# Maxima over key partitions: VectorE's 32x32 transposes and eight guard rows in place of TensorE's transposes and two guard rows

## The chip, the core and the metric

The kernel runs on one core of a Trainium2 chip. The core has five engines that work side by side, each through its own list of instructions in order: TensorE (PE, matmuls, with its weight loads shown as PEld), VectorE (DVE), ScalarE (ACT), GpSimd (POOL) and SyncE (SP, which here only issues DMAs). Data lie in SBUF, matmul results in PSUM's eight banks. The metric is the device time of one execution in microseconds (us).

## The reference

Four batches, eight heads, 768 positions, head dimension 64. Attention is masked by buckets: six projections of each query and key give six sign bits, and a query sees the keys with the same six bits. The result goes through a feed-forward layer (called MoE in the kernel).

```python
q_bits = (np.einsum('bhsd,dk->bhsk', q, proj) > 0)      # 6 bits; the same for k
mask = q_bucket[:, :, :, None] == k_bucket[:, :, None, :]
scores = scale * np.matmul(q, k.transpose(0, 1, 3, 2))
scores = np.where(mask, scores, -1000000000.0)
scores = scores - np.max(scores, axis=-1, keepdims=True)
attn = np.exp(scores)
attn = attn / (np.sum(attn, axis=-1, keepdims=True) + 1e-09)
out = np.matmul(attn, v)                                # then, over 3072 tokens of width 512:
h = x @ w_in                                            # 512 -> 2048
return (s * np.maximum(h, 0.0) ** 2 + b) @ w_out        # 2048 -> 512
```

## The kernel before

**Tiles and stages.** The attention is cut into 96 chunks: 4 batches x 8 heads x 3 chunks of 256 queries. For a chunk the scores are computed with keys on the partitions: six tiles of 128 keys by 256 queries, which fill three PSUM banks (0 to 2, or 5 to 7 in every second chunk of the first batch). Head dimension and hash bits are contracted together, so that masked pairs come out very low. The first batch (24 chunks, `exact`) multiplies in plain fp32 (`L576`, `L641`); the other three batches split each operand into two fp32r parts (`L578`, `L612`, `L643`, `L644`), and between their matmuls stand those of the MoE of the batch before (`L723`, `L740`), which can start when all heads of a batch are done. After the last chunk the MoE is alone. While the first batch runs, ScalarE, VectorE and GpSimd also decode the MoE's weights (`decode`, 32 units).

**The maxima.** Softmax needs the largest score of each query, over all keys, thus over partitions. Per chunk:
- `L583` (VectorE) takes the maximum over the six tiles: `mx`, 128 partitions x 256 queries.
- `L589` (TensorE) turns `mx` round with two 128x128 transposes into bank 4, queries on partitions.
- `L591` (VectorE) takes the maximum along each row, negated: `nmt`, 128 x 2.
- `L593` (TensorE) transposes `nmt` into 2 rows of 128 in bank 4.
- `L600` (VectorE) writes the guard rows: 2 rows of 256 columns, row j holding the negated maxima of queries j x 128 onward and zeros elsewhere. They lie in rows 0 and 1 of `bq` (`zhl` in the first batch).
- `L612` (`L610` in the first batch) adds them to the scores in PSUM: a matmul in whose stationary operand these rows are ones (`rest`).
- `L617` (ScalarE) takes the exponential, then come the sums (`L666`) and the value matmuls.

The rows of `bq` and `ks` that the guard rows take away are carried in `lead` (`L578`) instead, whose contraction is 64 + 12 + 2 = 78 rows.

**What sets the order.** `Plan` holds each step with an engine, a cost in us, the keys that it reads and writes and a priority, and `order` plays the steps through once with these costs: on each engine the step that is ready and has the lowest priority number goes next. Attention goes ahead of the MoE's matmuls, which fill what is left. `hold(4)` and `hold(None)` enclose steps that have bank 4 to themselves: the preparation of the next head's operands (`split`, `hash_`, `both`) uses it too. `decodes` says how many weight units are to be decoded by chunk i, by `FIRST` up to the eighth chunk and `RATE` after it. The emitted lists are fixed; on the chip each engine takes its list in order and waits where a result isn't there.

Of the kernel before, what the change touches and what calls it, by code (L numbers as in the profile page):

```python
# [173 lines left out]
def lsh_attention_moe(ctx: ExitStack, tc, q, k, v, proj, w_in, w_out, s, b, out):  # L174
# [89 lines left out]
    nmt = tile_("nmt", [P, 4, 2])  # L264
# [34 lines left out]
    pjh = tile_("pjh", [P, KB + MR], F32R)  # L299
    pjl = tile_("pjl", [P, KB + MR], F32R)  # L300
# [16 lines left out]
    ones = tile_("ones", [P, 1])  # L317
# [37 lines left out]
    def decode(u, pr):  # L355
# [53 lines left out]
    def thirds(g):  # L409
        return (0,) if g == 0 else (1, 2)  # L410
# [14 lines left out]
    def prep(w, i, pr):  # L425
# [28 lines left out]
        def split(g, i, pr):  # L454
            cols, o = slice(g * HS, (g + 1) * HS), bank[:, 4, 0:HS]

            def tr():
# [4 lines left out]
            act(HS, lambda: nc.scalar.activation(aq[:, cols], o, AF.Copy, scale=qk_sb), [("b", 4, "p")], AK(x, g=thirds(g)), pr, 0.12)
            dve(HS, lambda: nc.vector.scalar_tensor_tensor(bq[:, cols], o, qk_sb, f32(aq[:, cols]), ALU.mult, ALU.subtract), [("b", 4, "p")] + AK(x, g=thirds(g)), BK(x, g=thirds(g)), pr, 0.6)
            plan.hold(None)
            if g:
                dma(lambda: ks[0:D, 0], lambda: aq[D:P], AK(x, r=(1,)), KK(x, (0,)), pr, D * S * 4)
                dma(lambda: ks[TPC:D, 1], lambda: aq[D + TPC:P], AK(x, r=(1,)), KK(x, (3,)), pr, D * S * 4)
                dma(lambda: ks[HR:HR + TPC, 0], lambda: aq[D:D + TPC], AK(x, r=(1,)), KK(x, (4,)), pr, S * 4)
                dma(lambda: ks[D:P, 1], lambda: bq[D:P], BK(x, r=(1,)), KK(x, (1,)), pr, D * S * 4)

        def hash_(g, i, pr):
# [91 lines left out]
    def scores(i, pr):  # L563
# [41 lines left out]
        for p in range(NP_):
# [163 lines left out]
    def freed(x):  # L769
# [99 lines left out]
```

## Time and profile before

| | us |
|---|---|
| median of 3 runs (lowest, highest) | 1071.52 (1070.59, 1071.64) |
| the profiled execution | 1071.75 |
| its span in the trace | 1070.0 |
| TensorE busy | 1044.6 |
| ScalarE busy | 686.3 |
| GpSimd busy | 652.0 |
| VectorE busy | 634.7 |

Busy times are of the whole span. A matmul's time in the trace is that from its start to its end, with the length of the pipeline in it, and the next one starts before it ends; what an instruction costs TensorE is read from the starts of its neighbours. Where a row merges several instructions (x2, x6), its start is that of the first.

### The profile page before, as it was taken

The numbers are of one execution on the slowest core, as the hardware profiler recorded it, in microseconds if no ns is written. First come the engines' busy times: TensorE is split into PE (matmuls) and PEld (weight loads), VectorE is DVE, ScalarE is ACT, GpSimd is POOL, SyncE is SP. The second block draws the span as 40 slices with busy tenths as digits, with TensorE's granted clock in tenths as the row PEclk, the third lists the DMA queues.
The fourth block names the chain that finished last, engine by engine and source line by source line (L and its number), as shares of the span: only waits on it lengthen the run. The fifth ranks groups of instructions, "written<-read, shape, count | busy, mean of one in ns | idle before, by whom it ended". The sixth has DMA issues, their size and how long they took to land.

```text
span 1070.0 us, 18632 instructions
## 1 busy us (share of the span) xinstructions
PE 1044.6 (98%) x6918; PEld 936.2 (87%) x6918; DVE 634.7 (59%) x750; ACT 686.3 (64%) x1355; POOL 652.0 (61%) x593
## 2 busy tenths in 40 slices
PE   8999999889999999999999999999999999999998
PEld 6888788679999989899889999999899999988997
DVE  5676878757677676757676676767676765100000
ACT  4667778857677767666767676776767677333332
POOL 2355857767667676666757775767667777322221
PEclk9999999999999999999999999999999999999999
DMA  6344445322422332331342232242242130201010
GB/s 148 102 140 131 141 140 160 98 66 51 129 75 70 96 94 55 105 94 46 73 116 76 55 119 66 71 118 73 68 114 76 46 97 11 79 1 60 9 41 20
DMA packets 91402, 89.11 MB, mean 83 GB/s; under 512 B 61760, under 2 KB 65344, under 8 KB 91312
## 3 DMA queue, kind: packets, MB, share of 16 engines
q1 hardware_dynamic: 86112, 70.88, 24.8%
q10 hardware_dynamic: 5200, 17.05, 5.1%
q8 instruction: 54, 0.88, 0.3%
q14 instruction: 36, 0.29, 0.1%
HBM read 48.24 MB, written 18.87 MB: 63 GB/s over the span
## 4 chain that ended last, share of the span: by engine, by line
PE 87%; DMA 3%; POOL 3%; ACT 3%; issue 2%; DVE 2%; ACTq 0%; SPq 0%; DVEq 0%; POOLq 0%
PE bank L723 25%; PE bank L740 23%; PE bank L644 5%; PE bank L612 5%; PE bank L643 5%; PE bank L641 4%; PE bank L578 4%; PE bank L576 4%; PE bank L589 2%; DMA xd<-xsb 2%; PE bank L674 2%; PE bank L610 1%; PE bank L459 1%; POOL hl L637 1%; DMA raw<-in_moe_w_out_dram 1%
## 5 line engine op out<-in xcount | busy, mean ns | idle before, releaser
L637 POOL TENSOR_TENSOR hl<-et,hl 128x512 fp32r<-128x512 f32 x216 | 279.1, 1319 | 139.8 <-ACT hl L636 123.1
L723 PE MATMUL bank<-xc,w 128*128 128x256 f32 x2304 | 338.7, 285 | 1.1 <-DMA xc<-xd 0.7
L723 PEld LDWEIGHTS bank<-xc,w 128*128 128x128 f32 x2304 | 305.7, 191 | 9.3 <-DMA xc<-xd 0.9
L740 PE MATMUL bank<-w,ghb 128*128 128x512 f32 x768 | 258.9, 401 | 0.0
L731 POOL TENSOR_TENSOR glb<-rb,ghb 128x512 fp32r<-128x512 f32 x96 | 124.2, 1294 | 126.5 <-ACT ghb L730 110.4
L583 DVE TENSOR_REDUCE mx<-bank 128x256 f32<-128x1536 f32 x96 | 168.1, 1751 | 16.8 <-PE bank L578 12.2
L666 DVE TENSOR_REDUCE zb<-et 128x256 f32<-128x1536 f32 x72 | 126.0, 1750 | 50.0 <-ACT et L617 32.1
L740 PE MATMUL bank<-w,glb 128*128 128x512 f32 x384 | 153.5, 401 | 0.1
L617 ACT ACTIVATE et<-bank 128x512 f32<-128x512 f32 x240 | 132.5, 624 | 32.8 <-PE bank L612 21.0
L740 PEld LDWEIGHTS bank<-w,ghb 128*128 128x128 f32 x768 | 136.3, 189 | 17.9 <-issue 0.8
L728 ACT ACTIVATE rb<-bank 128x512 f32<-128x512 f32 x96 | 57.5, 599 | 144.6 <-PE bank L723 134.7
L636 ACT CAST hl<-et 128x512 fp32r<-128x512 f32 x216 | 131.4, 667 | 0.4
L643 PE MATMUL bank<-hl,vs 128*128 128x256 f32 x432 | 118.6, 294 | 1.0 <-ACT hl L636 0.6
L644 PE MATMUL bank<-hl,vs 128*128 128x256 f32 x432 | 113.8, 282 | 1.9 <-POOL hl L637 1.9
L679 ACT ACTIVATE xpb<-bank,vmn 64x256 f32<-64x256 f32 x96 | 44.9, 468 | 74.9 <-PE bank L644 74.0
L578 PE MATMUL bank<-aq,ks 78*128 78x256 f32 x432 | 86.8, 290 | 3.2 <-DMA aq<-nat 3.1
L644 PEld LDWEIGHTS bank<-hl,vs 128*128 128x128 f32 x432 | 82.3, 191 | 7.0 <-POOL hl L637 2.5
L643 PEld LDWEIGHTS bank<-hl,vs 128*128 128x128 f32 x432 | 82.1, 190 | 6.8 <-ACT hl L636 1.0
L686 DVE RECIPROCAL zpb<-zpb 128x256 f32<-128x256 f32 x48 | 83.5, 1741 | 5.3 <-ACT zpb L677 5.3
L740 PEld LDWEIGHTS bank<-w,glb 128*128 128x128 f32 x384 | 72.4, 189 | 11.7 <-POOL glb L731 0.6
L748 DVE SCALAR_TENSOR_TENSOR osb<-bank,misc,bcs 128x512 f32<-128x512 f32 x22 | 16.1, 741 | 109.2 <-PE bank L740 109.1
L578 PEld LDWEIGHTS bank<-aq,ks 78*128 78x128 f32 x432 | 69.8, 190 | 9.8 <-ACT zhl L667 3.3
(115 smaller groups left out, 1659.5 us busy)
## 6 DMA issues: line engine op xcount, KB each, us to landing
xd<-xsb SPq DMA_DIRECT2D x48, 256.0 KB
xc<-xd SPq DMA_DIRECT2D x48, 256.0 KB
raw<-in_moe_w_in_dram ACTq DMA_DIRECT2D x16, 512.0 KB
raw<-in_moe_w_out_dram ACTq DMA_DIRECT2D x16, 512.0 KB
nat<-in_q_dram SPq DMA_DIRECT2D x32, 192.0 KB
nat<-in_k_dram SPq DMA_DIRECT2D x32, 192.0 KB
out_dram<-osb SPq DMA_DIRECT2D x22, 256.0 KB
vn<-in_v_dram SPq DMA_DIRECT2D x24, 192.0 KB
```

Source lines behind the costliest of these rows:

```text
L578: nc.tensor.matmul(o, ks[0:HR + TPC, 0, kt], aq[0:HR + TPC, cs], start=m == 0, stop=m == 1, skip_group_check=True)
L583: dve(S * TPC, lambda: nc.vector.tensor_reduce(t, sc, AX.XY, ALU.max), [("b", b) for b in pb], [tk], pr, 1.75)
L617: act(512, lambda p=p, z=z: nc.scalar.activation(et(z) if plain(i) else pairs(z), bank[:, pb[p]] if plain(i) else bank[:, pb[p]].rearrange ...
L636: act(512, lambda z=z, y=y: nc.scalar.copy(HL[2 * y].rearrange("p (m n) -> p m n", n=CH), pairs(z)), [("e", z)], [("hl", 2 * y)], pr)
L637: pool(512, lambda z=z, y=y: nc.gpsimd.tensor_tensor(HL[2 * y + 1].rearrange("p (m n) -> p m n", n=CH), pairs(z), f32(HL[2 * y]).rearrange ...
L643: nc.tensor.matmul(av, VS[w % 2][:, kt], HL[2 * y][:, ms], start=(kt == 0), stop=False)
L644: nc.tensor.matmul(av, VS[w % 2][:, kt], HL[2 * y + 1][:, ms], start=False, stop=(kt == NT - 1))
L666: dve(S * TPC, lambda: nc.vector.tensor_reduce(ZB, es, AX.XY, ALU.add), [("e", z) for z in range(NE)], ["zb"], pr, 1.75)
L686: dve(CH, lambda: nc.vector.reciprocal(zp, zp), [], zk, pr + 20, 1.75)
L723: nc.tensor.matmul(hp, wt[("wi", n, cc)][:, m % 2, fs], xc[:, m // 2, :], start=(cc == 0 and m == 0), stop=(cc == NC_ - 1 and m == 2))
L731: pool(2 * CH, lambda r=r, gh=gh, gl=gl: nc.gpsimd.tensor_tensor(gl, r, f32(gh), ALU.subtract), [rk, hk], [lk], MP)
L740: nc.tensor.matmul(bank[:, 6 + t, :], (gh, gh, gl)[n][:, ts], wt[("wo", f)][:, n % 2], start=(f == 0 and n == 0), stop=(f == NF - 1 and n ...
```

## The change

The maxima over key partitions go another way. `mx` is transposed in place on VectorE in blocks of 32x32: a block of 32 keys by 32 queries becomes 32 queries by 32 keys. A reduction over each 32 columns gives `nmt`, 128 x 8: for each of four groups of 32 key partitions and eight groups of 32 queries the maximum over the keys of the group. One TensorE transpose makes 8 rows of 128 of it, a VectorE reduction over the four groups gives `qm`, 8 x 32, negated, and the product with the identity spreads it to 8 guard rows of 256 columns. The contraction in `lead` is 64 + 12 + 8 = 84 rows. Bank 4 is held from the small transpose to the reduction behind it. Besides, the keys by which the planner knows parts of `aq` and `bq` become finer, some planned costs and `FIRST` are other numbers, and three small tiles are laid together.

```diff
-    nmt = tile_("nmt", [P, 4, 2])
+    nmt = tile_("nmt", [P, NR])
+    QM = tile_("qm", [NR, SQ])
...
-        dve(256, lambda: nc.vector.tensor_scalar(raw()[:, :, 1], gi, -2**31, None, ALU.bitwise_and), [gk], rk, pr, 0.68)
-        dve(512, lambda: nc.vector.scalar_tensor_tensor(gi, gi, 3, raw()[:, :, 1], ALU.logical_shift_left, ALU.bitwise_or), rk, [gk], pr, 1.1)
+        dve(256, lambda: nc.vector.tensor_scalar(raw()[:, :, 1], gi, -2**31, None, ALU.bitwise_and), [gk], rk, pr, 0.6)
+        dve(512, lambda: nc.vector.scalar_tensor_tensor(gi, gi, 3, raw()[:, :, 1], ALU.logical_shift_left, ALU.bitwise_or), rk, [gk], pr, 0.92)
...
-        return (0,) if g == 0 else (1, 2)
+        return (0, 1) if g == 0 else (2, 3)
+
+    CG = ((0,), (1, 2), (3,))
...
-                dma(lambda: ks[TPC:D, 1], lambda: aq[D + TPC:P], AK(x, r=(1,)), KK(x, (3,)), pr, D * S * 4)
-                dma(lambda: ks[HR:HR + TPC, 0], lambda: aq[D:D + TPC], AK(x, r=(1,)), KK(x, (4,)), pr, S * 4)
+                dma(lambda: ks[NR:D, 1], lambda: aq[D + NR:P], AK(x, r=(1,)), KK(x, (3,)), pr, D * S * 4)
+                dma(lambda: ks[HR:HR + NR, 0], lambda: aq[D:D + NR], AK(x, r=(1,)), KK(x, (4,)), pr, S * 4)
...
-                dma(lambda: aq[HR:HR + TPC], lambda: bq[0:TPC], BK(x, r=(0,)), MK(x) + AK(x, r=(1,)), pr, S * 4)
+                dma(lambda: aq[HR:HR + NR], lambda: bq[0:NR], BK(x, r=(0,)), MK(x) + AK(x, r=(1,)), pr, S * 4)
...
-                    nc.tensor.matmul(o, ks[0:HR + TPC, 0, kt], aq[0:HR + TPC, cs], start=m == 0, stop=m == 1, skip_group_check=True)
+                    nc.tensor.matmul(o, ks[0:HR + NR, 0, kt], aq[0:HR + NR, cs], start=m == 0, stop=m == 1, skip_group_check=True)
...
+        m2, m2k = MX, "mx"
+        dve(CH, lambda: nc.vector.transpose(out=m2, in_=t), [tk], [m2k], pr, 0.33)
+        dve(CH, lambda: nc.vector.tensor_reduce(nm, m2.rearrange("p (b n) -> p b n", n=SQ), AX.X, ALU.max), [m2k], [nk], pr, 0.33)
         plan.hold(4)
...
-        def across():
-            for j in range(TPC):
-                nc.tensor.transpose(out=bank[:, 4, j * P:(j + 1) * P], in_=t[:, j * P:(j + 1) * P], identity=ident)
-        pe(0.23, across, [tk], [("b", 4, "c")], pr, True)
-        dve(CH, lambda: nc.vector.tensor_reduce(nm, bank[:, 4, 0:CH].rearrange("p (j n) -> p j n", j=TPC), AX.X, ALU.max, negate=True), [("b", 4, "c")], [nk], pr, 0.41)
-
-        pe(0.115, lambda: nc.tensor.transpose(out=bank[0:TPC, 4, 0:P], in_=nm, identity=ident), [nk], [("b", 4, "c")], pr, True)
+        pe(0.115, lambda: nc.tensor.transpose(out=bank[0:NR, 4, 0:P], in_=nm, identity=ident), [nk], [("b", 4, "c")], pr, True)
+        qm, qk = QM, "qm"
+        dve(CH, lambda: nc.vector.tensor_reduce(qm, bank[0:NR, 4, 0:P].rearrange("b (k n) -> b n k", n=SQ), AX.X, ALU.max, negate=True), [("b", 4, "c")], [qk], pr, 0.26)
+        plan.hold(None)
...
-            nc.vector.scalar_tensor_tensor(mr.rearrange("p (j n) -> p j n", j=TPC), o, -FLOOR, d, ALU.min, ALU.mult)
-        dve(CH, rows, [("b", 4, "c")], [mk], pr, 0.41)
-        plan.hold(None)
+            nc.vector.scalar_tensor_tensor(mr.rearrange("p (j n) -> p j n", j=NR), o, -FLOOR, d, ALU.min, ALU.mult)
+        dve(CH, rows, [qk], [mk], pr, 0.33)
...
-FIRST = 1.4
+FIRST = 1.6
```

The lines of the changed kernel that the rows below name: `L588` is the reduction `L583`, `L590` the block transpose, `L591` the reduction to `nmt`, `L595` the small transpose, `L597` the reduction to `qm`, `L605` the guard rows, `L616` the `rest` matmul; `L727` and `L744` are the MoE's matmuls, `L647` and `L648` the value matmuls, `L678` the sum's, `L690` the reciprocal.

On TensorE, the stretch from the small transpose to the guard rows' matmuls, in the third batch (the 66th chunk), before:

```order
L593 MATMUL bank<-ident,nmt 2x128
L740 MATMUL bank<-w_1325,ghb 128x512
L740 MATMUL bank<-w_1325,glb 128x512
L740 MATMUL bank<-w_1325,ghb 128x512 x2
L612 MATMUL bank<-bq_1320,ks_1496 128x256 x6
```

The same stretch of the same chunk in the changed kernel:

```order
L595 MATMUL bank<-ident,nmt 8x128
L727 MATMUL bank<-xc_1_2_4956,w_1422 128x256 x3
L727 MATMUL bank<-xc_1_3_4966,w_1434 128x256 x2
L678 MATMUL bank<-zhl,oner 128x256 x2
L727 MATMUL bank<-xc_1_3_4966,w_1434 128x256
L616 MATMUL bank<-bq_1337,ks_1518 128x256 x6
```

Four 512-column matmuls stood between the two; now eight of 256 columns do. The two transposes `L589` ahead of them are gone from the list.

On VectorE, the same chunk before:

```order
L583 TENSOR_REDUCE mx<-bank 128x256
L686 RECIPROCAL zpb<-zpb 128x256
L591 TENSOR_REDUCE nmt<-bank 128x2
L681 TENSOR_TENSOR xpb<-xpb,bank 64x256
L600 SCALAR_TENSOR_TENSOR bq_1320<-bank,ident 2x256
```

And in the changed kernel:

```order
L588 TENSOR_REDUCE mx<-bank 128x256
L590 STREAM_TRANSPOSE mx<-mx 128x256
L591 TENSOR_REDUCE nmt<-mx 128x8
L690 RECIPROCAL zpb<-zpb 128x256
L468 SCALAR_TENSOR_TENSOR bq_1337<-bank,misc,aq_1336 128x384
L685 TENSOR_TENSOR xpb<-xpb,bank 64x256
L597 TENSOR_REDUCE qm<-bank 8x32
L605 SCALAR_TENSOR_TENSOR bq_1337<-qm,ident 8x256
```

The reciprocal stood between the maxima and the reduction to `nmt`, where TensorE's two transposes ran; now it stands behind that reduction, with two other operations, where the small transpose runs.

On POOL, the end of the weights' decoding (`L377`, `L384`, `L385`) and the first low half of the second batch (`L637`), before:

```order
L377 TENSOR_TENSOR osb<-osb,raw_235 128x512
L385 TENSOR_TENSOR w_1610<-osb,w_1610 128x512
L687 TENSOR_TENSOR xpb<-xpb,zpb 128x256
L385 TENSOR_TENSOR w_1633<-osb,w_1633 128x512
L689 TENSOR_TENSOR xsb<-xpb,xsb 128x256
L384 TENSOR_TENSOR bcs<-bcs,osb 128x512
L637 TENSOR_TENSOR hl_1567<-et,hl_1561 128x512
```

And in the changed kernel, where the same operations are `L380`, `L387`, `L388` and `L641`:

```order
L387 TENSOR_TENSOR bcs<-bcs,osb 128x512
L691 TENSOR_TENSOR xpb<-xpb,zpb 128x256
L388 TENSOR_TENSOR w_1584<-osb,w_1584 128x512
L693 TENSOR_TENSOR xsb<-xpb,xsb 128x256
L691 TENSOR_TENSOR xpb<-xpb,zpb 128x256
L693 TENSOR_TENSOR xsb<-xpb,xsb 128x256
L691 TENSOR_TENSOR xpb<-xpb,zpb 128x256
L641 TENSOR_TENSOR hl_1575<-et,hl_1569 128x512
```

The last decode stood directly ahead of the first low half; now four other operations stand between.

## Rows read from the trace of the kernel before

**Rows 1.** The page: the line of part 1 (busy us, share of the span, instructions), and part 4, the chain that ended last by engine.

```profile
PE 1044.6 (98%) x6918; PEld 936.2 (87%) x6918; DVE 634.7 (59%) x750; ACT 686.3 (64%) x1355; POOL 652.0 (61%) x593
...
PE 87%; DMA 3%; POOL 3%; ACT 3%; issue 2%; DVE 2%; ACTq 0%; SPq 0%; DVEq 0%; POOLq 0%
```

**Rows 2.** Busy time of each engine by stage: start and end, length, then PE, PEld, DVE, ACT, POOL (instructions in brackets), the granted clock, DMA share and GB/s.

```profile
0.00:205.00 205.00, 194.92 (x1055) 161.22 (x1055) 148.26 (x213) 144.95 (x285) 117.67 (x106) 1.00 0.48 136
205.00:900.00 695.00, 683.30 (x4811) 625.31 (x4812) 473.95 (x521) 481.95 (x971) 488.13 (x450) 1.00 0.30 80
900.00:1070.00 170.00, 166.38 (x1056) 149.66 (x1054) 12.53 (x16) 59.37 (x100) 46.16 (x39) 1.00 0.10 35
```

**Rows 3.** Groups of instructions by line and shape: busy us and mean ns of one, then the idle time before them and what ended it.

```profile
L583 DVE TENSOR_REDUCE mx<-bank 128x256 f32<-128x1536 f32 x96 | 168.1, 1751 | 16.8 <-PE bank L578 12.2 <-PE bank L576 2.9 <-ACT hl L636 0.5
L666 DVE TENSOR_REDUCE zb<-et 128x256 f32<-128x1536 f32 x72 | 126.0, 1750 | 50.0 <-ACT et L617 32.1 <-ACT vmn L510 11.5 <-ACT zpb L677 3.0
L686 DVE RECIPROCAL zpb<-zpb 128x256 f32<-128x256 f32 x48 | 83.5, 1741 | 5.3 <-ACT zpb L677 5.3
L591 DVE TENSOR_REDUCE nmt<-bank 128x2 f32<-128x256 f32 x96 | 39.6, 412 | 57.3 <-PE bank L589 55.0 <-ACT zpb L677 2.1
L589 PE MATMUL bank<-ident,mx 128*128 128x128 f32 x192 | 37.3, 276 | 3.5 <-DVE mx L583 1.2 <-ACT hl L636 1.1 <-DVE bq L463 1.0
L600 DVE SCALAR_TENSOR_TENSOR bq<-bank,ident 2x256 fp32r<-2x256 f32 x72 | 29.4, 409 | 32.0 <-PE bank L593 31.5
L600 DVE SCALAR_TENSOR_TENSOR zhl<-bank,ident 2x256 fp32r<-2x256 f32 x24 | 9.8, 408 | 8.7 <-PE bank L593 8.2
L322 DVE CAST zhl<-zb 128x256 fp32r<-128x256 f32 x2 | 1.7, 858 | 0.0
L320 DVE MEMSET zb<- 128x256 f32 x1 | 0.3, 272 | 0.0
```

**Rows 4.** TensorE's instructions in order of time in two chunks of the third batch: start, us from start to end, line, count.

```profile
601.56 0.27 PE L593 MATMUL bank<-ident,nmt 128*2 128x128 f32 x1
...
609.40 0.28 PE L643 MATMUL bank<-hl,vs 128*128 128x256 f32 x1
609.52 0.28 PE L644 MATMUL bank<-hl,vs 128*128 128x256 f32 x1
609.64 0.38 PE L589 MATMUL bank<-ident,mx 128*128 128x128 f32 x2
609.78 0.36 PE L643 MATMUL bank<-hl,vs 128*128 128x256 f32 x1
609.98 0.28 PE L644 MATMUL bank<-hl,vs 128*128 128x256 f32 x1
...
611.97 0.27 PE L593 MATMUL bank<-ident,nmt 128*2 128x128 f32 x1
612.00 0.48 PE L740 MATMUL bank<-w,ghb 128*128 128x512 f32 x1
612.32 0.40 PE L740 MATMUL bank<-w,glb 128*128 128x512 f32 x1
612.55 0.63 PE L740 MATMUL bank<-w,ghb 128*128 128x512 f32 x2
```

**Rows 5.** VectorE's instructions in the same two chunks.

```profile
601.87 0.41 DVE L600 SCALAR_TENSOR_TENSOR bq<-bank,ident 2x256 fp32r<-2x256 f32 x1 [0.19 <-PE bank L593]
...
607.53 1.74 DVE L583 TENSOR_REDUCE mx<-bank 128x256 f32<-128x1536 f32 x1
...
610.86 0.35 DVE L591 TENSOR_REDUCE nmt<-bank 128x2 f32<-128x256 f32 x1
611.97 0.42 DVE L681 TENSOR_TENSOR xpb<-xpb,bank 64x256 f32<-64x256 f32 x1 [0.75 <-ACT xpb L679]
612.42 0.41 DVE L600 SCALAR_TENSOR_TENSOR bq<-bank,ident 2x256 fp32r<-2x256 f32 x1
```

**Rows 6.** The waits of TensorE's weight loads: who waited for whom, us in total, times, longest.

```profile
PEld bank L593 <- DVE nmt L591: 3.6, 7, 0.8
...
PEld bank L589 <- DVE mx L583: 2.3, 4, 1.3
...
PEld bank L612 <- DVE bq L600: 0.7, 3, 0.3
```

**Rows 7.** VectorE's instructions in order of time at 41 us: two of the weights' decoding, the second of which needs the first.

```profile
41.48 0.41 DVE L375 TENSOR_SCALAR raw<-osb 128x512 int32<-128x512 int32 x1
41.92 0.69 DVE L376 SCALAR_TENSOR_TENSOR osb<-osb,raw 128x512 int32<-128x512 int32 x1
```

**Rows 8.** All engines in order of time at 102 us, of which a product on VectorE and the weight load that waits for it.

```profile
102.07 0.41 DVE L600 SCALAR_TENSOR_TENSOR zhl<-bank,ident 2x256 fp32r<-2x256 f32 x1
...
102.53 0.31 PEld L445 LDWEIGHTS bank<-ident,nat 128*128 128x128 f32 x3 [0.50 <-DVE zhl L600]
```

**Rows 9.** The passage from the first to the second batch: POOL's instructions from 204 to 214 us, and the busy times from 205 to 235 us (columns as in rows 2).

```profile
204.42 1.74 POOL L377 TENSOR_TENSOR osb<-osb,raw 128x512 int32<-128x512 int32 x1 [0.83 <-DVE osb L376]
...
212.94 1.27 POOL L384 TENSOR_TENSOR bcs<-bcs,osb 128x512 f32<-128x512 f32 x1
214.16 2.60 POOL L637 TENSOR_TENSOR hl<-et,hl 128x512 fp32r<-128x512 f32 x2
...
205.00:235.00 30.00, 24.82 (x161) 21.83 (x162) 19.31 (x20) 20.12 (x41) 26.39 (x24) 0.97 0.28 72
```

More of the change, by code (lines that the diff above doesn't have):

```diff
@@ L185, in lsh_attention_moe @@
     TPC = CH // P
+    SQ = 32
+    NR = CH // SQ
     NC_ = DM // P
@@ L298, in lsh_attention_moe @@
             nc.vector.tensor_scalar(pj[rows, c:c + NBITS], pn[rows], (1.0 if i == r else -1.0) / (1.0 if i else SCALE), None, ALU.mult)
-    pjh = tile_("pjh", [P, KB + MR], F32R)
-    pjl = tile_("pjl", [P, KB + MR], F32R)
+    pjhl = tile_("pjhl", [P, 2, KB + MR], F32R)
+    pjh, pjl = pjhl[:, 0], pjhl[:, 1]
     nc.vector.tensor_copy(pjh, pj[:, 0:KB + MR])
@@ L316, in lsh_attention_moe @@
     nc.vector.memset(qk_sb[D:P], 1.0)
-    ones = tile_("ones", [P, 1])
+    ones = misc[:, 5:6]
     nc.vector.memset(ones, 1.0)
@@ L393, in bias, with AK, BK @@
         plan.hold(None)
-    def AK(x, r=(0, 1), g=(0, 1, 2)):
+    def AK(x, r=(0, 1), g=(0, 1, 2, 3)):
         return [("aq", x, i, j) for i in r for j in g]
-    def BK(x, r=(0, 1), g=(0, 1, 2)):
+    def BK(x, r=(0, 1), g=(0, 1, 2, 3)):
         return [("bq", x, i, j) for i in r for j in g]
@@ L582, in scores @@
+            pe(mmc(CH, 8 if exact else 2), lead, AK(x) + KK(x) if exact else AK(x, g=CG[c])  + KK(x, (0, 2, 4)), [("b", pb[p])], pr, True)
+        t, tk, nm, nk = MX, "mx", nmt, "nm"
         sc = bank[:, b0:b0 + NP_].rearrange("p b (m n) -> p n b m", n=CH)
         dve(S * TPC, lambda: nc.vector.tensor_reduce(t, sc, AX.XY, ALU.max), [("b", b) for b in pb], [tk], pr, 1.75)
+        m2, m2k = MX, "mx"
+        dve(CH, lambda: nc.vector.transpose(out=m2, in_=t), [tk], [m2k], pr, 0.33)
+        dve(CH, lambda: nc.vector.tensor_reduce(nm, m2.rearrange("p (b n) -> p b n", n=SQ), AX.X, ALU.max), [m2k], [nk], pr, 0.33)
@@ L600, in rows @@
-            nc.vector.scalar_tensor_tensor(mr.rearrange("p (j n) -> p j n", j=TPC), o, -FLOOR, d, ALU.min, ALU.mult)
-        dve(CH, rows, [("b", 4, "c")], [mk], pr, 0.41)
-        plan.hold(None)
+            mr = zhl[0:NR, y] if exact else bq[0:NR, cs]
+            o = qm.rearrange("p (j n) -> p j n", j=1).broadcast_to([NR, NR, SQ])
+            d = ident[0:NR, 0:NR].rearrange("p (j n) -> p j n", n=1).broadcast_to([NR, NR, SQ])
+            nc.vector.scalar_tensor_tensor(mr.rearrange("p (j n) -> p j n", j=NR), o, -FLOOR, d, ALU.min, ALU.mult)
@@ L612, in rest @@
                     nc.tensor.matmul(o, ks[:, 1, kt], bq[:, cs], start=False, stop=m == 1, skip_group_check=True)
-            pe(mmc(CH, 2), rest, [mk, tk] + ([] if exact else BK(x, g=(c,)) + KK(x, (1, 3))), [("b", pb[p])], pr, True)
+            pe(mmc(CH, 2), rest, [mk, tk] + ([] if exact else BK(x, g=CG[c]) + KK(x, (1, 3))), [("b", pb[p])], pr, True)
         ES = [(npiece[0] + p) % (NE + 2 * NHL) for p in range(NP_)] if plain(i) else list(range(NP_))
```

11 lines of the change are left out of this document (3 added, 8 removed).

## The prediction

> **What bounds the kernel.** I read the page first, its busy shares and the chain that ended last: TensorE is busy 98% of the span and 87% of the chain runs through it, 2% through VectorE [rows 1]. Then the windows by stage [rows 2]: up to 205 us (the first batch, 24 chunks) TensorE is busy 195 of 205 us and VectorE 148; from 205 to 900 us (72 chunks, with matmuls of the MoE between them) 683 of 695 and 474; from 900 us the MoE is alone, TensorE 166 of 170, VectorE 13. The granted clock is 1.00 in all three. So TensorE's queue sets the end: whatever TensorE does not have to issue between 205 and 900 us lets MoE matmuls come forward, and the lone MoE at the end gets shorter by it. VectorE matters only where TensorE, which works through its list in order, comes to an instruction whose VectorE result isn't there. That is rare now: TensorE's weight loads wait for `L583` 2.3 us in 4 cases, for `L591` 3.6 us in 7, at `L612` for `L600` 0.7 us in 3, all of 96 or 72 chunks [rows 6].
>
> **What goes from TensorE.** Two 128x128 transposes per chunk (`L589`, 192 in all [rows 3]). Their price is not the mean of 276 ns, which holds the pipeline's length, but what they push back [rows 4]: from `L589` at 609.64 to the second instruction behind it at 609.98 pass 0.34 us, of which the `L643` between takes 0.12 (as from 609.40 to 609.52). The pair costs 0.22 us. 96 x 0.22 = 21.1 us; 24 of the 96 lie in the first stage, 72 in the second (the two rows of `L600` [rows 3]). The small transpose stays (`L593`, now `L595`): 8 columns loaded in place of 2, the same 128 moved; 0.12 us in [rows 4] (611.97 to 612.32, less 0.23 for the `L740`). The scores contract over 84 rows instead of 78; `L578` and `L612` differ more than that in rows and start 0.12 us apart like all 256-column matmuls, so nothing.
>
> **What VectorE gets.** Per chunk it loses `L591` (0.41) and `L600` from PSUM (0.41) [rows 3]. It gets a 32x32-block transpose of 128x256, a reduction of 128x256 from SBUF, one of 8x128 from PSUM and a product of 8x256 from SBUF. Rows: the reductions of 1536 columns from PSUM (`L583`) and SBUF (`L666`) take the same 1.75 us, and 1.75 less 0.41 over 1280 columns is 1.05 ns a column. So 256 columns from SBUF are 0.41, 128 from PSUM 0.41 - 0.13 = 0.28, the product 0.41. No row shows the block transpose. Its ends are the fill of the same tile shape, 0.27 (`L320`), and the cast of that shape, 0.86 (`L322`); I take 0.41, what this trace's one-pass operations on 256 columns have. A VectorE operation that needs the one before it starts some 0.03 us after its end (`L375` ends at 41.89, `L376` starts at 41.92 [rows 7]). Together 1.51 for 0.82 us: +0.69 x 96 = 66 us on VectorE, 635 to 701 us, 66% of the span; in the second stage 474 + 50 of 695, 75%. TensorE hides that, as long as VectorE isn't late at the two places where TensorE needs it.
>
> **First place: from the column maxima to the small transpose.** (`L590`, new `L591`, `L595`, `L597`, `L605` and `L616` are lines of the changed kernel.) The planner is told 0.33 + 0.33 us for the transpose and the reduction; by the rows it is 0.03 + 0.41 + 0.03 + 0.41 = 0.88, late by 0.22. Queued behind `L595` on TensorE are the MoE and the value matmuls that hide everything else. In the chunk shown `L583` ends at 609.27 and TensorE takes `L589` at 609.64 [rows 4, 5], 0.37 us later, so a lateness of 0.22 would have been swallowed; the 4 waits in 96 [rows 6] say that such slack is usual. I choose 0.04 us a chunk, the whole 0.22 in one chunk of five or six.
>
> **Second place: from the small transpose to the guard row's matmuls.** Before, `L593` starts at 601.56 in the chunk before, `L600` 0.31 later at 601.87 [rows 4, 5]; it takes 0.41, and a waiting weight load goes 0.05 after its end (102.48 to 102.53 [rows 8]): 0.77 in all. The order rows put four `L740` (4 x 0.23) and the transpose's own 0.12 ahead of `L612`: 1.04, slack 0.27. After, 0.31 + 0.28 + 0.03 + 0.41 + 0.05 = 1.08 are needed, and the order rows show eight 256-column matmuls and the transpose ahead of `L616`: 9 x 0.12 = 1.08. No slack is left, so that every further tenth that VectorE is late is paid. I choose 0.05 us a chunk, an estimate. Both places: 0.09 x 96 = 8.6 us; bounds 0 (if the operations are as short as the planner has them; `L591` is 0.35 in one case [rows 5]) and 39 (the slow rival).
>
> [...]
>
> **What else.** The waits at `L589` itself, 3.5 us of TensorE [rows 3], go with it; their cause, a VectorE result that comes late, stays for `L595`, so I take 2 back (bounds 0 and 3.5). `FIRST` 1.6 decodes the MoE weights sooner. Before, POOL still decodes from 204 to 214 us in front of the first `L637` of the second batch, the first and the last of six operations in the rows, and TensorE loses 5.2 of the 30 us from 205 to 235 [rows 9]; the order rows show four other operations between the last decode (`L388`) and that first `hl` (`L641`) now, where there was none. I take 3 back (0 to 5.2). Bank 4 is held from the small transpose to the reduction only; the rows show one wait for it, `L445` behind `L600`, 0.50 us [rows 8], and it would end some tenths sooner: nothing that counts. The finer keys for the halves of `aq` and `bq` bind only the preparation of the next head, which the planner places after the chunks that read them: nothing. Of three DMAs per head on SP's queue, two carry 8 rows in place of 2 (6 x 768 x 4 bytes, 18 KB more) and one 6 rows fewer, beside copies of 196 KB: nothing.
>
> Sum: 1071.75 (the profiled execution) - 21.1 + 8.6 - 2 - 3 = 1054.2; it stands 0.2 above the median of the runs, so 1054.0.
>
> **The rivals.**
> 1. Short operations: VectorE's new operations cost what the planner has, no wait appears. 1071.5 - 21.1 - 2 - 3 = 1045. For it: the 0.35 us of `L591` at 610.86. Against: its mean of 0.41 [rows 3]. [...]
> 2. Queueing: `L597` stands on VectorE behind the reciprocal (1.74 us [rows 3]) and two more in the order rows, where `L600` stood behind one, `L681`. If one of these runs late, the bank-4 result lies there and `L616` waits. 0.15 us more a chunk: 1054 + 14 = 1068. For it: `L600` at 612.42 came 0.1 us late because of `L681` [rows 5]. Against: VectorE has a quarter of its time left.
> 3. Slower: the block transpose is slow. At 0.86 the first place needs 0.03 + 0.86 + 0.03 + 0.41 = 1.33 where the planner has 0.66, 0.67 late; less the 0.31 of slack in [rows 4, 5] (0.37 without the 0.06 of a handover) TensorE stands 0.36 at `L595` in each chunk, and 0.05 at `L616`: 0.41 x 96 = 39, which gives 1071.5 - 26 + 39 = 1084. It decides from 0.27 us of new waits a chunk, where the 26 us are eaten. For it: no row shows the operation. Against: both one-pass reductions run at 1.05 ns a column.
> [...]
> 4. No change: what TensorE saves turns into waits for the MoE's data or VectorE. TensorE's second stage has 12 us of idle in 695, so there is always an MoE matmul to take; little speaks for it.
>
> **The numbers.** Forecast 0.50 (own range 1047 to 1061), short 0.18, queueing 0.13, slower 0.14, no change 0.05. About 0.2% is what a measurement of this kernel can tell, 2 us. Faster by more: 0.50 + 0.18 + 0.13 less a little of the queueing case = 0.80; within: 0.05; slower: 0.15. The range 1042 to 1073 leaves out the slow end and a gain of all the waits.
>
> **What would show it.** Right: TensorE's work falls by 21 us and the lone MoE after the last chunk starts about as late as before (some 900 us) but is shorter; `L590` and `L591` at 0.41; TensorE waits at `L595` and `L616` some 5 to 12 us in sum; less idle of TensorE from 205 to 235. Wrong: `L590` above 0.6, or waits at these two above 26 us in sum, or a first stage that grows by more than 5 us because VectorE, 72% busy there, falls behind.

## The result, and the profile after

| | us | ratio to the kernel before, 95% interval |
|---|---|---|
| forecast | 1054.0 (1042 to 1073) | |
| changed kernel, median of 4 (lowest, highest) | 1080.25 (1079.41, 1081.46) | 1.0082 (1.0068 to 1.0097) |
| kernel before, median of 4 | 1071.58 (1070.59, 1072.36) | |

The changed kernel is slower by 8.7 us, where 17.5 us less were forecast. The first lines answer to [rows 1]: the busy times of the changed kernel, and the chain that ended last by engine and by line.

```profile
PE 1037.6 (96%) x6726; PEld 917.6 (85%) x6726; DVE 745.1 (69%) x942; ACT 687.2 (64%) x1355; POOL 657.1 (61%) x593
...
PE 69%; DVE 16%; ACT 6%; POOL 4%; issue 4%; DMA 1%; ACTq 0%; DVEq 0%; POOLq 0%
PE bank L727 21%; PE bank L744 18%; PE bank L616 5%; DVE bq L605 4%; PE bank L583 4%; PE bank L645 3%; PE bank L648 3%; PE bank L647 3%; PE bank L581 3%; DVE mx L588 3%; ACT et L621 2%; POOL hl L641 2%; DVE zb L670 1%; DVE zpb L690 1%; PE bank L614 1%
```

TensorE has 192 instructions fewer, as the change says, but the span grew: its idle time went from 25.4 us (1070.0 - 1044.6) to 42.1 (1079.7 - 1037.6). Its share of the chain fell from 87% to 69%, and 16% now run through VectorE, which had 2%: the first VectorE line among them is `L605`, the guard rows. VectorE's busy time is 110 us more, where 66 were forecast. By stage, with the columns of [rows 2]:

```profile
0.00:205.00 205.00, 191.13 (x998) 155.52 (x998) 173.93 (x262) 145.32 (x286) 125.53 (x111) 0.99 0.49 138
205.00:900.00 695.00, 671.22 (x4622) 604.34 (x4623) 557.14 (x664) 479.70 (x965) 482.20 (x442) 1.00 0.30 80
900.00:1079.70 179.70, 175.29 (x1109) 157.78 (x1107) 14.07 (x18) 62.14 (x104) 49.35 (x42) 1.00 0.09 33
```

From 205 to 900 us TensorE's idle doubled, from 11.7 to 23.8 us. The attention ends when it did (the last chunk's maxima start at 896.6 us, before at 896.1), and the lone MoE at the end is 10 us longer, where the forecast's 72 chunks of 0.22 us would have made it some 16 shorter. The groups that answer to [rows 3] (busy us and mean ns of one) say which VectorE operation grew:

```profile
L605 DVE SCALAR_TENSOR_TENSOR bq<-qm,ident 8x256 fp32r<-8x256 f32 x72 | 62.2, 863 | 2.5
L590 DVE STREAM_TRANSPOSE mx<-mx 128x256 f32<-128x256 f32 x96 | 42.7, 445 | 3.2
L591 DVE TENSOR_REDUCE nmt<-mx 128x8 f32<-128x256 f32 x96 | 40.3, 420 | 3.3
...
L597 DVE TENSOR_REDUCE qm<-bank 8x32 f32<-8x128 f32 x96 | 25.8, 268 | 31.3 <-PE bank L595 30.3
...
L605 DVE SCALAR_TENSOR_TENSOR zhl<-qm,ident 8x256 fp32r<-8x256 f32 x24 | 15.0, 623 | 0.9
```

Three of the four new operations came within 0.04 us of their price (0.41, 0.41, 0.28). The product `L605` takes 0.86 and 0.62 us on average instead of 0.41. Its line in the trace has 411 ns at the least, 925 in the median and 1599 at the most in the last three batches. The waits of TensorE's weight loads, which answer to [rows 6], are at the place that needs it:

```profile
PEld bank L616 <- DVE bq L605: 34.9, 55, 1.3
PEld bank L614 <- DVE zhl L605: 6.2, 8, 1.5
...
PEld bank L595 <- DVE nmt L591: 0.8, 4, 0.3
```

They were 0.7 at `L612` and 1.5 at `L610`, 2.2 us in all, and are 41.1 now. In part of such a wait the matmul before still runs; TensorE's own idle time at `L616` is the figure behind the bar, 20.8 us, where it was 0.0 at `L612`:

```profile
L616 PE MATMUL bank<-bq,ks 128*128 128x256 f32 x432 | 69.3, 296 | 20.8 <-DVE bq L605 20.4
```

What the product waits for is read from two chunks, VectorE's, POOL's and TensorE's instructions in order of time, of one chunk at 445 us and one at 475 us:

```profile
445.04 0.28 DVE L597 TENSOR_REDUCE qm<-bank 8x32 f32<-8x128 f32 x1 [0.67 <-PE bank L595]
445.35 1.43 DVE L605 SCALAR_TENSOR_TENSOR bq<-qm,ident 8x256 fp32r<-8x256 f32 x1
...
475.93 0.41 DVE L605 SCALAR_TENSOR_TENSOR bq<-qm,ident 8x256 fp32r<-8x256 f32 x1
...
445.22 1.28 POOL L735 TENSOR_TENSOR glb<-rb,ghb 128x512 fp32r<-128x512 f32 x1
...
474.69 0.73 POOL L672 TENSOR_TENSOR zhl<-zb,zhl 128x256 fp32r<-128x256 f32 x1
477.15 1.00 POOL L542 TENSOR_TENSOR vs<-vn,vs 128x384 fp32r<-128x384 f32 x1 [1.73 <-ACT vs L541]
...
445.65 0.28 PE L648 MATMUL bank<-hl,vs 128*128 128x256 f32 x1
446.83 0.97 PE L616 MATMUL bank<-bq,ks 128*128 128x256 f32 x6 [0.90 <-DVE bq L605]
```

At 475.93 POOL rests and the product takes 0.41. At 445.35 POOL has been in `L735` since 445.22; that ends at 446.50, the product at 446.78, 0.28 behind it. TensorE stands 0.90 us at `L616`. `L605` is not waiting for a semaphore there: its operand `qm` is done at 445.32, and its time counts as busy. It multiplies `qm` by `ident`, both in SBUF; `L600` before had one operand in PSUM and took 0.35 to 0.41 in all 96 chunks, in 67 of them beside POOL. The two chunks stand for all: in the 27 where POOL is in no instruction when the product starts, the product takes 0.411 to 0.417 us. In the other 69 it takes 0.411 to 1.599, 0.96 on average, and ends 0.27 to 0.33 us behind an instruction of POOL; in the longest cases that is the second of two.

In the chunk shown POOL is first, and 1.15 of `L735`'s 1.28 us lie in the product's 1.43. What in the chip makes the one end behind the other, the trace doesn't show; whether it hangs on where the operand lies is tried in runs 1 and 2. The trace shows the other order too, VectorE's line first and then POOL's:

```profile
865.14 0.41 DVE L605 SCALAR_TENSOR_TENSOR bq<-qm,ident 8x256 fp32r<-8x256 f32 x1
...
865.15 1.56 POOL L735 TENSOR_TENSOR glb<-rb,ghb 128x512 fp32r<-128x512 f32 x1 [0.42 <-ACT ghb L734]
```

Here the product started 0.01 us sooner and took its 0.41, and POOL's operation took 1.56. The 13 instances of `L735` that start inside a product have a median of 1.48 us, the 83 others 1.29.

The trace of before held the price already, in an operation that I had shown for another reason [rows 7]. `L376` (128x512) also has two operands in SBUF. Its group:

```profile
L376 DVE SCALAR_TENSOR_TENSOR osb<-osb,raw 128x512 int32<-128x512 int32 x32 | 28.5, 892 | 0.6
```

And VectorE and POOL in order of time around two of its instances:

```profile
46.89 1.74 DVE L376 SCALAR_TENSOR_TENSOR osb<-osb,raw 128x512 int32<-128x512 int32 x1
...
42.75 1.29 POOL L377 TENSOR_TENSOR osb<-osb,raw 128x512 int32<-128x512 int32 x1 [3.38 <-issue]
46.79 1.30 POOL L385 TENSOR_TENSOR w<-osb,w 128x512 fp32r<-128x512 f32 x1 [2.75 <-ACT w L379]
```

The instance at 41.92 in [rows 7], with POOL idle until 42.75, took 0.69; the one at 46.89, with POOL in `L385` until 48.09, took 1.74. The group's mean of 892 against that 0.69 is the mark of it.

### The profile page after: what moved, and what is told of

Its sections match the earlier page's. It is cut to its first block, busy times and chain, and to the rows that moved or that the text cites. A ratio compares the mean times of both kernels' runs of the same rounds, so it can differ in the third digit from the quotient of the medians.

```text
span 1079.7 us, 18383 instructions
## 1 busy us (share of the span) xinstructions
PE 1037.6 (96%) x6726; PEld 917.6 (85%) x6726; DVE 745.1 (69%) x942; ACT 687.2 (64%) x1355; POOL 657.1 (61%) x593
## 4 chain that ended last, share of the span: by engine, by line
PE 69%; DVE 16%; ACT 6%; POOL 4%; issue 4%; DMA 1%; ACTq 0%; DVEq 0%; POOLq 0%
PE bank L727 21%; PE bank L744 18%; PE bank L616 5%; DVE bq L605 4%; PE bank L583 4%; PE bank L645 3%; PE bank L648 3%; PE bank L647 3%; PE bank L581 3%; DVE mx L588 3%; ACT et L621 2%; POOL hl L641 2%; DVE zb L670 1%; DVE zpb L690 1%; PE bank L614 1%
## 5 line engine op out<-in xcount | busy, mean ns | idle before, releaser
L641 POOL TENSOR_TENSOR hl<-et,hl 128x512 fp32r<-128x512 f32 x216 | 279.2, 1319 | 117.2 <-ACT hl L640 94.2
L727 PE MATMUL bank<-xc,w 128*128 128x256 f32 x2304 | 331.4, 284 | 0.1
L727 PEld LDWEIGHTS bank<-xc,w 128*128 128x128 f32 x2304 | 303.8, 191 | 7.2 <-ACT rb L732 0.7
L744 PE MATMUL bank<-w,ghb 128*128 128x512 f32 x768 | 256.7, 398 | 0.0
L735 POOL TENSOR_TENSOR glb<-rb,ghb 128x512 fp32r<-128x512 f32 x96 | 126.0, 1312 | 129.8 <-ACT ghb L734 119.4
L588 DVE TENSOR_REDUCE mx<-bank 128x256 f32<-128x1536 f32 x96 | 168.1, 1751 | 4.5 <-PE bank L581 2.5
L744 PE MATMUL bank<-w,glb 128*128 128x512 f32 x384 | 152.6, 398 | 0.0
L744 PEld LDWEIGHTS bank<-w,ghb 128*128 128x128 f32 x768 | 136.3, 189 | 17.5
L648 PE MATMUL bank<-hl,vs 128*128 128x256 f32 x432 | 113.8, 284 | 2.2 <-POOL hl L641 2.0
L647 PE MATMUL bank<-hl,vs 128*128 128x256 f32 x432 | 115.1, 287 | 0.0
L648 PEld LDWEIGHTS bank<-hl,vs 128*128 128x128 f32 x432 | 81.9, 190 | 8.9 <-POOL hl L641 4.0
L616 PE MATMUL bank<-bq,ks 128*128 128x256 f32 x432 | 69.3, 296 | 20.8 <-DVE bq L605 20.4
L583 PE MATMUL bank<-aq,ks 84*128 84x256 f32 x432 | 87.4, 289 | 0.0
L690 DVE RECIPROCAL zpb<-zpb 128x256 f32<-128x256 f32 x48 | 83.6, 1742 | 5.3 <-ACT zpb L681 5.1
L616 PEld LDWEIGHTS bank<-bq,ks 128*128 128x128 f32 x432 | 56.0, 189 | 35.8 <-DVE bq L605 34.9
L647 PEld LDWEIGHTS bank<-hl,vs 128*128 128x128 f32 x432 | 81.8, 189 | 5.3 <-issue 0.2
```

Of the source, the lines that this page charges most:

```text
L583: nc.tensor.matmul(o, ks[0:HR + NR, 0, kt], aq[0:HR + NR, cs], start=m == 0, stop=m == 1, skip_group_check=True)
L616: nc.tensor.matmul(o, ks[:, 1, kt], bq[:, cs], start=False, stop=m == 1, skip_group_check=True)
L641: pool(512, lambda z=z, y=y: nc.gpsimd.tensor_tensor(HL[2 * y + 1].rearrange("p (m n) -> p m n", n=CH), pairs(z), f32(HL[2 * y]).rearrange ...
L647: nc.tensor.matmul(av, VS[w % 2][:, kt], HL[2 * y][:, ms], start=(kt == 0), stop=False)
L648: nc.tensor.matmul(av, VS[w % 2][:, kt], HL[2 * y + 1][:, ms], start=False, stop=(kt == NT - 1))
L727: nc.tensor.matmul(hp, wt[("wi", n, cc)][:, m % 2, fs], xc[:, m // 2, :], start=(cc == 0 and m == 0), stop=(cc == NC_ - 1 and m == 2))
```

## The experiments

In the diffs the lines are those of the changed kernel where nothing else is said.

**1 and 2. Where the product's operand lies.** So that no other step of the plan uses bank 4 while `qm` lies there, the hold is lengthened in both runs; then `qm` is put into PSUM in the second. The lists of all engines are the same in both.

```diff
-        ... negate=True), [("b", 4, "c")], [qk], pr, 0.26)
-        plan.hold(None)
+        ... negate=True), [], [("b", 4, "c"), qk], pr, 0.26)
...
-        dve(CH, rows, [qk], [mk], pr, 0.33)
+        dve(CH, rows, [qk, ("b", 4, "c")], [mk], pr, 0.33)
+        plan.hold(None)
```

> Control for the next run: the changed kernel, with bank 4 held until the guard rows' product is done instead of until the reduction before it; all operands stay where they are (qm in SBUF). Theory A (the product, L605, has both its tensor operands in SBUF and is held up while POOL runs one of its own tensor operations): the product stays at 0.8 us on average between 0.41 and 1.6, TensorE waits for it some 35 us at its weight loads as in the changed kernel, 1080 +- 4 us. Theory B (the chain of four VectorE operations is too long as such, wherever its operands are): the same, 1080. Theory C (how long bank 4 is held decides): a change by more than 5 us, up or down.

And for the second run also:

```diff
-        qm, qk = QM, "qm"
+        qm, qk = bank[0:NR, 4, P:P + SQ], "qm"
```

> As the control, instruction for instruction in the same order on every engine, but qm lies in bank 4 in PSUM, so that the product reads one operand from PSUM and one from SBUF, as it did before the change. Theory A: every one of the 96 products takes 0.41 us whatever POOL does, the waits of TensorE's weight loads at the guard rows' matmuls fall from 41 us to below 10, and the time to 1050 to 1056 us (the forecast's sum). Theory B: the product gets shorter, but TensorE still waits, since transpose and reduction are late by 0.2 us each chunk; the time falls by less than 10 us, to 1070 to 1078.

Measured: 1084.73 us with `qm` in SBUF (ratio to before 1.0127, 1.0097 to 1.0157), 1057.64 with `qm` in PSUM (0.9872, 0.9848 to 0.9896). The product's group in the control, then its two groups in the run with PSUM, and the waits of the weight loads there:

```profile
L604 DVE SCALAR_TENSOR_TENSOR bq<-qm,ident 8x256 fp32r<-8x256 f32 x72 | 59.9, 832 | 2.5
```

```profile
L604 DVE SCALAR_TENSOR_TENSOR bq<-bank,ident 8x256 fp32r<-8x256 f32 x72 | 29.6, 412 | 2.5
L604 DVE SCALAR_TENSOR_TENSOR zhl<-bank,ident 8x256 fp32r<-8x256 f32 x24 | 9.9, 412 | 0.9
```

```profile
PEld bank L616 <- DVE bq L604: 4.7, 15, 1.0
...
PEld bank L614 <- DVE zhl L604: 3.3, 6, 1.1
```

(`L604` is `L605` here.) With the same lists and one operand elsewhere, every product takes 0.41 us (0.411 to 0.414), the waits fall to 8.0 us and 27 us of time go. Theory A holds for the product and the waits; the time is 1.6 us above the range that it had given. The forecast's 1054 is missed by 3.6 us once the product costs what it had been given, but that nearness is in part luck, as the last paragraph of the next section shows. Theory B is not dead by this: the next runs show that the rest of the chain costs too. The longer hold by itself is not the gain; the control is slower than the changed kernel, by 4.5 us in the medians, with wide intervals, and 0.7 above the range that was expected of it.

**3. The product at its real price in the plan.**

```diff
-        dve(CH, rows, [qk], [mk], pr, 0.33)
+        dve(CH, rows, [qk], [mk], pr, 0.86)
```

> The changed kernel with the planned cost of the product at 0.86 us (its measured mean in batches two to four) instead of 0.33; operands in SBUF as in the changed kernel. If the time is lost because TensorE's list brings the guard rows' matmuls up too early (lists out of step with the chip): the list now has 0.5 us more of other matmuls ahead of them, the waits at their weight loads fall from 41 us to about 15 and the time to 1060 to 1066. If it is lost because the chain itself is longer and chunks come later, whatever the list: the waits go elsewhere and the time stays within 4 us of 1080.

Measured: 1068.46 us (0.9976, 0.9960 to 0.9992). The wait at `L616` in its trace:

```profile
PEld bank L616 <- DVE bq L605: 11.1, 24, 0.7
...
PEld bank L595 <- DVE nmt L591: 6.0, 23, 0.5
```

The product is as slow as before (mean 835 ns in the last three batches), but TensorE has other matmuls ahead, the wait falls from 34.9 to 11.1 and 12 us come back. That is about half of the 22.6 us between the changed kernel and run 2: this half comes of a list that brings `L616` up too early, and not of VectorE's time as such. It stops short of the 1060 to 1066 that was expected. Part of the wait went to the small transpose, where TensorE's loads now wait 6.0 us for `L591` instead of 0.8. That a time which swings between 0.41 and 1.6 can't be planned by one number may be the rest; no run shows that.

**4 and 8. `FIRST` alone**, in the changed kernel (1.6 to 1.4) and in the kernel before (1.4 to 1.6).

```diff
-FIRST = 1.6
+FIRST = 1.4
```

> The changed kernel with FIRST back at 1.4, all else as changed. By the forecast's term for the earlier decoding (3 us gained, bounds 0 to 5): 1083, with TensorE idle 1 to 5 us more between 205 and 235 us. If the decoding's pace is without effect: within 2 us of 1080. If it costs (decoding beside a VectorE that is fuller in the first stage, and more of POOL's operations beside the products there): 1077 or below.

> The kernel before with FIRST at 1.6 alone. No product with two operands from SBUF in the guard rows here, so the pace of decoding is seen by itself. Forecast's term: 3 us faster (0 to 5). If FIRST 1.6 costs by itself: up to 5 us slower. If it is without effect: within 2 us of the kernel before on this chip.

Measured: 1075.21 us, 5.0 below the changed kernel; and 1076.34 for the kernel before with 1.6, against 1070.87 for it on that chip (ratio 1.0049, 1.0032 to 1.0065). The term has the wrong sign in both. Busy times of 50 to 150 us of the kernel before (its passage is in [rows 9]):

```profile
50.00:150.00 100.00, 98.22 (x538) 81.75 (x536) 74.33 (x93) 76.22 (x151) 62.90 (x53) 1.00 0.45 132
```

then of 50 to 150 us and of the passage with `FIRST` 1.6:

```profile
50.00:150.00 100.00, 95.77 (x520) 79.43 (x519) 80.75 (x96) 77.06 (x152) 71.10 (x57) 1.00 0.46 142
205.00:235.00 30.00, 26.12 (x152) 22.08 (x150) 16.90 (x20) 17.57 (x39) 15.96 (x17) 0.89 0.20 58
```

The decoding now stands between 50 and 150 us, where VectorE gets 6 and POOL 8 us more, and TensorE loses 2.4. In the passage TensorE is busy 1.3 us more (24.8 to 26.1), but with 152 instructions instead of 161 and a granted clock of 0.89 instead of 0.97: the busy time per instruction is 0.172 us instead of 0.154, and this is no gain. The clock is also lower over the whole run: 0.992 to 0.995 in the four executions, 0.995 to 0.998 in the seven of the kernel before, of which those at 0.998 take some 2 us less than those at 0.995. With medians of 0.995 and 0.997, some 1.5 of the 5.5 us may be the clock; this is an estimate. The rest has no place in this reading and stays open.

In the changed kernel the passage did gain. First with `FIRST` 1.6, then with 1.4:

```profile
205.00:235.00 30.00, 27.87 (x186) 24.41 (x187) 23.91 (x28) 19.91 (x41) 16.21 (x16) 1.00 0.21 59
```

```profile
205.00:235.00 30.00, 24.25 (x148) 20.38 (x149) 21.31 (x26) 21.57 (x43) 25.94 (x24) 0.94 0.28 70
```

That is 3.6 us more for TensorE with 1.6, and 38 instructions. But the product is also slower with 1.6, 0.86 us against 0.74 in the last three batches, and the waits at the guard rows are 41.1 us against 32.5, so that this pair doesn't tell the pace of decoding from the luck of meeting POOL.

**5 to 7. `FIRST` and the plan's costs once the operand is in PSUM.** All three start from run 2; `psum14` has `FIRST` 1.4, `psum_costs` the measured costs, `psum_costs14` both.

```diff
-        dve(CH, lambda: nc.vector.transpose(out=m2, in_=t), [tk], [m2k], pr, 0.33)
+        dve(CH, lambda: nc.vector.transpose(out=m2, in_=t), [tk], [m2k], pr, 0.48)
...
-        ... AX.X, ALU.max), [m2k], [nk], pr, 0.33)
+        ... AX.X, ALU.max), [m2k], [nk], pr, 0.45)
...
-        ... negate=True), [], [("b", 4, "c"), qk], pr, 0.26)
+        ... negate=True), [], [("b", 4, "c"), qk], pr, 0.28)
...
-        dve(CH, rows, [qk, ("b", 4, "c")], [mk], pr, 0.33)
+        dve(CH, rows, [qk, ("b", 4, "c")], [mk], pr, 0.44)
```

> The run with qm in PSUM and FIRST back at 1.4. If the forecast's term for the earlier decoding holds (3 us gained): 1060 to 1062 us against 1057.6. If FIRST 1.6 costs by itself the 5 us that its undoing gave in the changed kernel: 1052 to 1054. If those 5 us came by another hit rate of the product and POOL's operations (the product's mean was 0.74 there against 0.86), they are gone now that the product takes 0.41 everywhere: within 2 us of 1057.6.

> The run with qm in PSUM, and the planner given what the trace shows: block transpose 0.48 (0.445 and the start behind it), reduction 0.45, reduction to qm 0.28, product 0.44, instead of 0.33, 0.33, 0.26, 0.33. If the remaining lateness of the chain against the list costs what the forecast has (8.6 us for both places): about 1050 us, and the waits of TensorE's weight loads at the small transpose and at the guard rows' matmuls fall from 16 us to under 6. If its list absorbs the lateness already: 1056 to 1059.

> Both: qm in PSUM, measured costs, FIRST 1.4. With the forecast's terms: 1053. With FIRST costing 5 us by itself and lateness 8: 1045. With neither of effect: 1056 to 1059.

| | `FIRST` 1.6 | `FIRST` 1.4 |
|---|---|---|
| planned costs as in the change | 1057.64 | 1056.55 |
| measured costs | 1041.22 | 1036.69 |

The ratios to the kernel before are 0.9862 (0.9848 to 0.9877) for `psum14`, 0.9723 (0.9709 to 0.9738) for `psum_costs` and 0.9681 (0.9666 to 0.9695) for `psum_costs14`, the fastest of all. The measured costs are worth 16.4 and 19.9 us, twice what the forecast had for both places together. `FIRST` 1.6 costs 4.5 us with the measured costs. Without them it is 1.1, which the spread of the runs doesn't tell from nothing; that was the third reading expected of `psum14`, that the 5.0 us in the changed kernel came of how often the product met POOL. The 4.5 us have a place, the first 205 us, where TensorE is busy 3.4 us less with 1.6 than with 1.4. First `psum_costs`, then `psum_costs14`, the latter also from 205 to 900 us:

```profile
0.00:205.00 205.00, 191.22 (x1000) 156.52 (x1001) 170.29 (x263) 147.08 (x287) 124.80 (x111) 0.99 0.49 140
```

```profile
0.00:205.00 205.00, 194.60 (x1021) 161.49 (x1021) 169.34 (x264) 147.97 (x290) 120.25 (x110) 0.99 0.48 139
205.00:900.00 695.00, 693.42 (x4873) 637.30 (x4874) 532.07 (x670) 498.89 (x997) 499.25 (x461) 1.00 0.31 82
```

The page of `psum_costs14`, and its waits at the two places:

```profile
PE 1020.0 (98%) x6726; PEld 917.9 (89%) x6726; DVE 706.1 (68%) x942; ACT 689.5 (67%) x1355; POOL 649.9 (63%) x593
```

```profile
PEld bank L614 <- DVE zhl L604: 4.0, 7, 1.1
PEld bank L595 <- DVE bq L468: 1.6, 2, 1.3
...
PEld bank L616 <- DVE bq L604: 0.8, 2, 0.4
```

TensorE's idle is 15.6 us (1035.6 less 1020.0), 9.8 less than before the change, and its busy time 24.6 less. The idle time went between 205 and 900 us: 1.6 us there (695 less 693.4) against 11.7 before, of which the passage from 205 to 235 us has 1.1 against 5.2. VectorE works 71 us more than before the change and is 68% busy, and it costs nothing that these lines show.

**9 and 10. Which of the costs.** `psum_front14` has only the two costs ahead of the small transpose (0.48, 0.45), `psum_back14` only the two behind it (0.28, 0.44); both from `psum14`.

> qm in PSUM, FIRST 1.4 (1056.6 before this edit), and of the measured costs only those ahead of the small transpose: block transpose 0.48, reduction 0.45 instead of 0.33 each. Both pairs of costs together gave 1036.7. If the lateness at the first place (0.27 us against the list) carries the 20 us: 1037 to 1042. If the second place carries them: 1053 to 1057.

> The other half: qm in PSUM, FIRST 1.4, and only the costs behind the small transpose as measured: reduction to qm 0.28, product 0.44 instead of 0.26 and 0.33. If the first place carries the 20 us: 1053 to 1057. If the second place does, whose slack the forecast put at zero: 1037 to 1042. If both are needed: both halves near 1047.

Measured: 1050.00 us (0.9805, 0.9788 to 0.9823) and 1048.03 (0.9786, 0.9771 to 0.9801): 6.6 and 8.5 us, together 15.1 of the 19.9. Neither place carries it alone. That answers to the third case of the second expectation.

**11. A control for the list.** The kernel before, with 0.54 planned for `L591` and `L600` in place of 0.41, which is what they take.

> A control: the kernel before, whose planned costs of the reduction to nmt and of the guard rows (0.41) are what the trace shows, with 0.54 planned for both. If any list with more room in this chain is faster, whether or not the costs were too low: 5 us or more faster than before. If the gain of the measured costs came from lateness against the list, there is none here: within 3 us of before, or slower.

Measured: 1067.29 us (0.9964, 0.9952 to 0.9977), 3.7 us faster. So room in this chain beyond its real length is worth something by itself, a little more than I had allowed; it is a fifth of what the right costs brought in the changed kernel. It lies between the two cases that were expected. The two edits add 0.26 us of room to the chain here and the measured costs 0.40 us there; at the rate seen here some 6 of those 16 to 20 us would be room as such, an estimate. Whether room beyond the measured costs would help the changed kernel too was not tried.

**12. Less decoding at the start still.** `psum_costs14` with `FIRST` 1.2.

> qm in PSUM, measured costs, FIRST 1.2 (1036.7 at 1.4, 1041.2 at 1.6). If more decoding in the first chunks costs time there, as 1.6 against 1.4 does, and nothing is lost later: 1032 to 1036. If 1.4 lies where both ends meet, the decoding left over for the passage to the second batch (205 to 235 us) costs what the start gains: 1036 to 1042, with TensorE's idle in that passage up by 2 to 5 us.

Measured: 1040.37 us (0.9712, 0.9696 to 0.9728), 3.7 above 1.4. In the passage TensorE is 28.8 of 30 us busy against 28.9 there, so the second reading fits in the time and not in its place. The place is again the first 205 us, where TensorE is busy 190.8 us against 194.6. 1.4 is the best of the three.

## Why the prediction was wrong

- **What goes from TensorE, 21.1 us:** nothing speaks against it. The version without the later mistakes (`psum_costs14`) is 34 us faster than before, of which 24.6 are busy time of TensorE; no run takes the transposes out alone.
- **What VectorE gets:** transpose 0.445, reduction 0.420, reduction to `qm` 0.268 against 0.41, 0.41, 0.28. **The step that failed is "the product 0.41".** I took it from `L600`, which reads PSUM, without asking what changes when the operand moves to SBUF. It takes 0.41 for certain only when POOL rests at its start (0.411 to 0.417 us in 27 chunks): 0.863 on average in 72 chunks and 0.623 in 24, (0.863 - 0.411) x 72 + (0.623 - 0.411) x 24 = 38 us of VectorE, all of them ahead of a matmul for which TensorE waits. Moving that operand back is worth 27 us (runs 1 and 2). Added to the forecast of 1054 that gives 1081, by a sum whose other terms were off too.
- **The second place:** found to be without slack, "every further tenth that VectorE is late is paid", and that is what happened: 41.1 us of waits at `L616` and `L614`, 0.43 a chunk instead of the 0.05 chosen, and above the 26 us that the prediction named as a sign of being wrong. The slow rival's point of decision, 0.27 us of new waits a chunk, fits; its mechanism (a slow block transpose, late at the first place) did not show. The transpose is nearly as fast as taken (0.445 for 0.41), and `L595` waits 0.8 us for `L591`.
- **Both places, 8.6 us:** mis-sized. With the product at 0.41 the costs that the plan has too low are worth 16 to 20 us (runs 5 to 7). I counted only the waits that the listing shows. With each of them TensorE, as I read it, also loses the overlap with the matmul before, and that stands in its busy time (1032.7 in run 2, 1020.0 in `psum_costs14`); a part of this difference may be the granted clock (0.995 against 0.998, between which the kernel before differs by some 2 us), and that the lost overlap is the rest wasn't tried.
- **`FIRST`, 3 us gained:** wrong in sign. In the changed kernel the gain in the passage came, 3.6 us, in the kernel before it did not; in both I priced only the place that the decoding left, and not the first 205 us, to which it went.
- **The other edits at nothing** (the 84 rows, the DMAs): nothing in the trace speaks against it, and the `lead` matmuls of 84 rows start 0.12 us apart in the median, as those of 78 did (not all 256-column matmuls do, as the prediction has it: those in plain fp32, `L576`, start 0.22 us apart). They weren't tried by themselves. The queueing rival's lateness is there, but it is not what was paid: `L597` starts over 0.40 us behind `L595` in 33 of 96 chunks, in 15 of them right behind the reciprocal, 21 us late in sum against the usual 0.31 (16 chunks and 6.5 us for `L600` before). That is the rival's 0.15 us a chunk. Run 2 has 23 us of it and waits only 8.0 us at the guard rows, whatever their cause.

From the fastest run upward the medians are: 1036.7, with `FIRST` 1.6 1041.2 (+4.5), with the plan's costs too low 1057.6 (+16.4), with the product's operand in SBUF and the shorter hold 1080.25 (+22.6). Beside the forecast's terms this shows the luck in the 3.6 us: `FIRST` was 7.5 us worse than forecast (4.5 lost, 3 gained) and the costs 7.8 worse (16.4 for 8.6), but what is left without both is a gain of 34.8 us where 23.1 were forecast, 11.7 better. What stays open is why the fastest run is 34 us below the kernel before, when the transposes are worth 21 and the room in the list some 4. Of the 9.8 us of TensorE's idle that went with it, 4.1 left the passage; no run takes apart what ended the rest.

## What to carry to other kernels

When an edit moves an operand from PSUM to SBUF, count the SBUF operands of the instruction and see what POOL does at that time: an instruction of the same form with two SBUF operands, whose mean in the trace lies well above its shortest, shows the price (in the kernel before `L376`, 892 ns against 668; the product of the changed kernel then had 863 against 411). Where a fixed list sets the order, put in the durations that a trace shows: four costs that were 0.40 us too low in sum, in a chain that the busiest engine waits for, cost 16 to 20 us over 96 rounds here, although the listing of waits looked small. Work that is moved out of a bad stretch has to be priced in the stretch that it enters, and a busy time is to be read with the granted clock and the count of instructions beside it.

## What was not expected of the hardware

A VectorE product of 8x256, 0.411 to 0.417 us with POOL at rest at its start, took up to 1.60 us beside POOL's tensor operations when both its operands lay in SBUF, and 0.411 to 0.414 in all 96 cases with one of them in PSUM. In all 69 chunks where POOL's operation was there first it ended 0.27 to 0.33 us after one of POOL's. In the other order it is POOL's operation that gets longer, 1.56 us in the instance shown, 1.48 in the median of the 13 such instances of `L735`, against 1.29 in that of the 83 others. The wait is booked as busy time of VectorE, so that neither the idle columns nor the list of waits show it on VectorE.
